# Bias rows first, spatial weights earlier, output weights later, and the gate's tail tile moved forward

## The chip, the core and the metric

The kernel runs on one core of a Trainium2 chip. A core has a matmul engine (PE, with its weight loads shown apart as PEld), a vector engine (DVE), a scalar engine (ACT), GpSimd (POOL), and a queue engine (SP) that only issues transfers. Each works through its own instructions in order, and semaphores tie them together. Matmuls read from on-chip memory (SBUF) and write to accumulator banks (PSUM), which DVE and ACT empty. The metric is the time of one execution on the device in microseconds (us).

## The reference

An attention with eight batches, eight heads, 576 positions and head size 64, followed by a gated layer with a spatial product. Cut to what matters:

```python
scores = scale * q @ k.T
bias = -(cum[:, None] - cum[None, :])          # cum = cumsum(max(s, 0))
scores = where(causal, -1e9, scores + minimum(bias, 0))
x = softmax(scores) @ v                        # heads joined: 576 x 512
h = maximum(x @ w_in, 0)                       # 576 x 1024
u, v = h[..., :512], h[..., 512:]
v_n = (v - mean(v)) / sqrt(var(v) + 1e-6)
v_s = w_spatial @ v_n + b_spatial[:, None]
out = (u * v_s) @ w_out
```

## The kernel before

Every number is held as a sum of two 16-bit halves, so a product is three matmuls. The 576 positions are four tiles of 128 and a tail of 64.

*Attention.* Heads go in pairs, four pairs to a batch, 32 in all. `s_pass` makes the scores of a pair (L303) with DVE's maximum (L307) and ACT's exponential (L313), splits the weights into halves (L322 on ACT, L323 on DVE) and transposes them through SP's queue (L328, `pT`, and `pT('t', p)` for the tail rows). `av_pass` multiplies them with V (L401, and L408 for the tail) and writes the operand `xt` of the second part (L415 on ACT, L416 on DVE). The tail columns of `xt`, from 512 on, come from `avt`, once per batch after its fourth pair. The operands of a pair come by POOL's queue (`raw`) and are split by L241 to L250. Pairs 0 to 2 take their scores from unsplit operands, for which `native_cum` copies the running sums into `kraw` (L128); pair 3 is the first that is split.

*Gated layer, `mlp(b)`.* For each batch 29 steps of PE: five tiles of the gate (`vps`, L443: four full ones and the tail), eight products for u (`ups`, L494), eight spatial products (`sps`: L507 with the full tiles, L509 with the tail's halves `vx`, L510 with the tail's first half and the three bias rows in `VY`), and eight output products (`ops`, L529). A gate tile is emptied by ACT (L459, `hv`), has its mean and variance taken by DVE (L463, L467), is normalized (POOL L469 and L470, DVE L471) and split (ACT L477, DVE L478) into `vn1` and `vn2`. The tail tile is computed in two halves of 64 rows; these exchange their statistics by two transfers on SP (L465, L466), and its result goes by six more (L482 to L484) to `vx` and `VY`. All spatial products of a batch need all five tiles. In batch 0 two gate tiles are begun ahead (`early` is 2); in the others `early` is 0.

*Weights.* They come in chunks of 128 rows. Input and output weights are 64-bit numbers that DVE unpacks in four steps (L167, L168, L170, L174) with one square on ACT (L173); `split_w` makes the halves (ACT L148, then either DVE L150 or ACT L152 and POOL L153). The output weights' chunks come by POOL's queue into one buffer, `wst`. The spatial weights (`load_wsp`) take L148 and L150. `load_wtail` loads the 64 rows of the tail twice into `wsx_st`, splits them into `wx1` and `wx2`, makes three 16-bit pieces of the bias with six steps on DVE (L203, L205, L207) in buffers of tags `ob` and `wst`, and writes them by SP to rows 64 to 66 of `wx2` (L209).

*Order.* PE runs in the order in which the program is written: a plan of (position, step), sorted. Position 2p is the start of pair p, and batch b's 29 steps stand at 8b + 10.3 to 8b + 18.3. The orders of the other engines and the queues are made from the same plan by a scheduler when the program is built; up to position 12.416 a step that is not first waits in its engine's order for the last step that is. The pool of gate, u, spatial and output banks has three, and `hv` has two buffers.

Of the kernel before, what the change touches and what calls it, by code (L numbers as in the profile page):

```python
# [11 lines left out]
AF = mybir.ActivationFunctionType  # L12
ALU = mybir.AluOpType
# [6 lines left out]
SWSP = 1024.0  # L20
SVN = 64.0
# [9 lines left out]
def attn_gated_mlp(ctx, tc, kqT, v, s, w_in, w_spT, b_sp, w_out, outT):  # L31
    nc = tc.nc
# [4 lines left out]
    NH = B * H  # L37
# [8 lines left out]
    NFULL = S // P  # L46
    TAIL = S - NFULL * P
    NC5 = NFULL + 1
# [47 lines left out]
    s_raw, s_pos, cum, zer = (cst[:, i * S:(i + 1) * S] for i in range(4))  # L96
# [14 lines left out]
    engs = (nc.gpsimd.tensor_copy, nc.vector.tensor_copy, nc.scalar.copy)  # L111
# [13 lines left out]
    def native_cum(pair):  # L125
        k = raws[pair // 2, 2 * (pair % 2), "k"]
        for j in range(2):
            engs[(N_C5, N_C5, N_C3, N_C4)[pair]](k[0:NH, j], cum)  # L128

    def init_static(i):  # L130

# [12 lines left out]
    wx1 = cp.tile([P, S], F16, name="wx1")  # L144
    wx2 = cp.tile([P, S], F16, name="wx2")

    def split_w(dst1, dst2, raw, sc, dve):
        nc.scalar.activation(dst1, raw, AF.Copy, bias=0.0, scale=sc)  # L148
        if dve:
            nc.vector.scalar_tensor_tensor(out=dst2, in0=raw, scalar=sc, in1=dst1, op0=ALU.mult, op1=ALU.subtract)  # L150
            return
        nc.scalar.activation(raw, raw, AF.Copy, bias=0.0, scale=sc)  # L152
        nc.gpsimd.tensor_tensor(out=dst2, in0=raw, in1=dst1, op=ALU.subtract)  # L153
# [41 lines left out]
    def load_wtail():  # L195
        s4 = wk.tile([P, S], F32, tag="ob", bufs=2, name="wsx_st")
        nc.sync.dma_start(out=s4[0:TAIL], in_=w_spT[NFULL * P:S])
        nc.sync.dma_start(out=s4[TAIL:2 * TAIL], in_=w_spT[NFULL * P:S])
        split_w(wx1, wx2, s4, SWSP, N_W3 > 4)
        bf = wk.tile([1, S], F32, tag="ob", bufs=2, name="bf")  # L200
        bp = wk.tile([1, 3, S], F16, tag="wst", bufs=1, name="bp")
        nc.sync.dma_start(out=bf, in_=b_sp)
        nc.vector.tensor_scalar(bf, bf, SWSP * SVN / 2048.0, None, op0=ALU.mult)  # L203
        for i in range(3):
            nc.vector.tensor_copy(bp[:, i], bf)  # L205
            if i < 2:
                nc.vector.tensor_tensor(out=bf, in0=bf, in1=bp[:, i], op=ALU.subtract)  # L207
        for i in range(3):
            nc.sync.dma_start(out=wx2[TAIL + i:TAIL + i + 1], in_=bp[:, i])  # L209


    def aux_rows(p):
# [207 lines left out]
    def mlp(b):  # L420
# [11 lines left out]
        def gate_mm(t, cs):  # L432

            tail = t == NFULL
            w = NF // 2 if tail else NF
            if 0 in cs:
                banks[t] = psM.tile([P, 512], F32, tag="M", name=f"vps{b}_{t}")
            ps = banks[t]
            for c in cs:
                for n, (xx, ww) in enumerate(((x1, win1), (x1, win2), (x2, win1))):  # L440
                    for g in range(2 if tail else 1):
                        m = slice(64 * g, 64 * g + 64) if tail else slice(0, P)
                        nc.tensor.matmul(ps[m, 0:w], xx[:, c, t * P:t * P + (m.stop - m.start)],  # L443
                                         ww[:, c, NF + g * w:NF + g * w + w],
                                         start=c == n == 0, stop=c == KC - 1 and n == 2)

        early = N_GP if b == 0 else 0
        if early:
            for c in range(KC - 1):
                for t in range(early):  # L450
                    gate_mm(t, range(c, c + 1))
                yield
        for t in range(NC5):
            tail = t == NFULL
            w = NF // 2 if tail else NF
            gate_mm(t, range(KC - 1 if t < early else 0, KC))
            ps = banks.pop(t)
            hv = wk.tile([P, NF], F32, tag="hv", bufs=2, name=f"hv{b}_{t}")[:, 0:w]
            nc.scalar.activation(hv, ps[:, 0:w], AF.Relu, bias=0.0, scale=VSCALE)  # L459
            st = wk.tile([P, 2, 6], F32, tag="st", bufs=2, name=f"st{b}_{t}")  # L460
            mv = wk.tile([P, 2], F32, tag="mv", bufs=2, name=f"mv{b}_{t}")
            rs = wk.tile([P, 1], F32, tag="rs", bufs=2, name=f"rs{b}_{t}")
            nc.vector.bn_stats(out=st[:, 0], in_=hv)  # L463
            if tail:
                nc.sync.dma_start(out=st[0:64, 1], in_=st[64:128, 0])  # L465
                nc.sync.dma_start(out=st[64:128, 1], in_=st[0:64, 0])  # L466
            nc.vector.bn_aggr(out=mv, in_=st if tail else st[:, 0])  # L467

            nc.gpsimd.tensor_scalar(rs, mv[:, 1:2], 1.0e-6, 1.0 / (SVN * SVN), op0=ALU.add, op1=ALU.mult)  # L469
            nc.gpsimd.tensor_tensor(out=rs, in0=rs, in1=mhalf, op=ALU.pow)  # L470
            nc.vector.tensor_scalar(hv, hv, mv[:, 0:1], rs, op0=ALU.subtract, op1=ALU.mult)  # L471
            if tail:
                d1 = wk.tile([P, w], F16, tag="th", bufs=1, name=f"th{b}")
                d2 = wk.tile([P, w], F16, tag="tl", bufs=1, name=f"tl{b}")
            else:
                d1, d2 = vn1[:, t], vn2[:, t]
            nc.scalar.copy(d1, hv)  # L477
            nc.vector.tensor_tensor(out=d2, in0=hv, in1=d1, op=ALU.subtract)  # L478
            if tail:
                for g in range(2):  # L480
                    m, gs = slice(64 * g, 64 * g + 64), slice(g * w, g * w + w)
                    nc.sync.dma_start(out=vx[0:TAIL, gs], in_=d1[m])  # L482
                    nc.sync.dma_start(out=vy[0:TAIL, gs], in_=d1[m])
                    nc.sync.dma_start(out=vx[TAIL:P, gs], in_=d2[m])  # L484
            yield
# [13 lines left out]
        for hf in range(2):  # L499
            for f in range(FC):  # L500
# [4 lines left out]
                for c in range(NFULL):  # L505
                    for vv, ww in ((vn1, ws1), (vn1, ws2), (vn2, ws1)):
# [6 lines left out]
                                               in1=u[:, f, ts], op0=ALU.mult, op1=ALU.mult)  # L513
# [31 lines left out]
    def at(pos, first, fn, *args):  # L545
        plan.append((pos, len(plan), first, fn, args))
# [19 lines left out]
    at(-20, True, native_sel, 0)  # L566
    at(-19.95, True, prefix_sums)
    at(-19.9, True, native_cum, 0)
    at(-19, True, native_tiles, 1)
    at(-19, True, native_sel, 1)  # L570
    at(-18.9, True, native_cum, 1)
    at(0.5, True, behind, "c", load_raw, 3)
    at(0.6, True, init_static, 0)
    at(0.6, True, behind, "c", fetch_v, 0)
# [4 lines left out]
    at(2.1, True, native_tiles, 2)  # L579
    at(2.1, True, native_sel, 2)  # L580
    at(3, True, native_cum, 2)
    at(5, True, init_static, 1)
    at(5, True, init_static, 2)
# [11 lines left out]
    for c in range(KC):  # L595
        at(2.2 + 1.2 * c, False, fetch_win, 1, c)
        at(4.5 + c, False, fetch_win, 0, c)
        at(6.5 + 0.5 * c, False, load_win, 1, c)
        at(9 + 0.5 * c, False, load_win, 0, c)
        at(11 + 0.4 * c, False, load_wsp, c)  # L600
        at(10.6 + 1.1 * c, False, load_wout, c)
    at(13, False, load_wtail)
    for p in range(NP):
        units([2 * p + k / 3 for k in range(6)], p < 4, s_pass, p)
        at_av = 2 * p + 3.72 if p != 3 else 9.4
        units([at_av, at_av + 0.35], p < 4, av_pass, p)
    for b in range(B):
        poss = [8 * b + 10.3 + 8 / NU * k for k in range(NU)]
        if b == 0:
            pre = [7.3, 8.25, 8.75]  # L610
            units(pre + poss, lambda k: k < len(pre), mlp, b)
        else:
            units(poss, False, mlp, b)
# [54 lines left out]
```

## Time and profile before

| | |
|---|---|
| median of 2 runs | 735.51 us (734.78 to 736.24) |
| profiled execution | 734.97 us |
| its span | 733.2 us |
| PE busy | 600.2 us, 82% |
| DVE busy | 607.0 us, 83% |
| ACT busy | 520.9 us, 71% |
| POOL busy | 226.0 us, 31% |

The profile's page cuts the span into 40 slices of 18.3 us and gives the busy share of each in tenths:

```profile
PE   4474375741998899889989889997999898999997
DVE  8889999795879899789979898999789897985531
POOL 9105465451123432342225331432034322100100
PEclk9788577995999999999999999999999999999999
```

In the first nine slices PE is busy between 30 and 79%, while the weights are loaded and unpacked beside the first pairs, and DVE 70% and more. The tenth slice (about 165 to 183 us) stands out: PE at one tenth, its clock at five. From slice 11 on PE is busy 80 to over 90%, until the last slice.

In the views that follow, a row of the timeline gives start, duration, engine, line, operation, what is written and read, sizes and count; in brackets stands how long the engine was idle before it and what released it. Line numbers are those of the kernel before. After the change lines behind L199 are 4 or 5 higher.

### The profile page before, as it was taken

The page shows a single profiled execution, that of the slowest core. Times are in us where ns is not written, and L with a number is a line of the kernel's source. Part 1 is how long each engine was busy: PE and PEld are TensorE (multiplying, and loading weights), DVE is VectorE, ACT ScalarE, POOL GpSimd, SP SyncE. Part 2 cuts the span into 40 slices and gives each one's busy share as a digit, 9 for nine tenths or more (in the row PEclk, how much of TensorE's full clock was granted, in tenths as well). Part 3 has the DMA queues.
Part 4 walks back from the last instruction along what each step waited for, and adds up shares of the span by engine and source line. Part 5 has one row for each costly group of instructions (what it writes and reads, how often), then busy time and mean ns, then how long its engine had stood idle before and what let it go on. Part 6 is the DMA issues. An engine that isn't in the chain of part 4 may idle for free. (4 is left out here: it accounts for less than half of the span.)

```text
span 733.2 us, 15915 instructions
## 1 busy us (share of the span) xinstructions
PE 600.2 (82%) x5696; PEld 415.7 (57%) x5696; DVE 607.0 (83%) x1660; ACT 520.9 (71%) x1328; POOL 226.0 (31%) x303
## 2 busy tenths in 40 slices
PE   4474375741998899889989889997999898999997
PEld 2152132531774677466756666565756665777576
DVE  8889999795879899789979898999789897985531
ACT  4787578663678777877877868786788787875322
POOL 9105465451123432342225331432034322100100
PEclk9788577995999999999999999999999999999999
DMA  8997747866279597967797698969986979465001
GB/s 224 289 201 132 199 99 198 171 176 156 56 169 202 131 180 181 209 136 160 177 191 161 159 163 184 211 128 167 206 200 123 178 131 179 99 107 123 32 13 64
DMA packets 235101, 114.81 MB, mean 157 GB/s; under 512 B 213471, under 2 KB 216717, under 8 KB 235022
## 3 DMA queue, kind: packets, MB, share of 16 engines
q1 hardware_dynamic: 225726, 78.74, 57.2%
q0 software_dynamic: 9296, 35.07, 16.5%
q8 instruction: 44, 0.72, 0.4%
q14 instruction: 35, 0.29, 0.1%
HBM read 37.28 MB, written 9.44 MB: 64 GB/s over the span
## 5 line engine op out<-in xcount | busy, mean ns | idle before, releaser
L313 ACT ACTIVATE p<-psS,mx 128x256 f32<-128x256 f32 (+3 forms) x256 | 132.9, 524 | 72.5 <-DVE mx L307 57.9
L250 POOL TENSOR_TENSOR QB<-raw,QA 64x288 f16<-64x288 f32 x116 | 118.4, 1049 | 213.2 <-ACT QA L246 175.9
L307 DVE CUSTOM_DVE_ANT_0 psS<-psS,mb 128x512 f32<-128x512 f32 (+2 forms) x320 | 154.3, 493 | 14.2 <-PE psS L303 12.0
L323 DVE SCALAR_TENSOR_TENSOR pb<-p,sm,pb 128x384 f16<-128x384 f32 (+3 forms) x256 | 134.8, 559 | 2.1 <-ACT pb L322 1.6
L322 ACT ACTIVATE pb<-p,sm 128x384 f16<-128x384 f32 (+3 forms) x256 | 122.8, 555 | 7.0 <-DVE sm L318 3.2
L443 PE MATMUL vps<-win,xt 128*128 128x512 f16 (+1 forms) x576 | 105.2, 354 | 18.6 <-ACT ob L532 9.6
L303 PE MATMUL psS<-KA,QA 128*128 128x128 f16 (+1 forms) x348 | 82.9, 312 | 40.4 <-ACT p L313 37.7
L507 PE MATMUL sps<-ws,vn 128*128 128x288 f16 x768 | 106.7, 289 | 10.8 <-DVE g L512 7.2
L494 PE MATMUL ups<-xt,win 128*128 128x288 f16 x768 | 106.6, 293 | 0.6 <-ACT u L497 0.4
L529 PE MATMUL ops<-g,wo 128*128 128x288 f16 x768 | 101.8, 286 | 1.1 <-DVE g L515 1.0
L507 PEld LDWEIGHTS <-vn 128*128 128x128 f16 x768 | 74.6, 99 | 35.9 <-issue 13.2
L494 PEld LDWEIGHTS <-win 128*128 128x128 f16 x768 | 75.6, 100 | 28.7 <-issue 5.1
L303 PE MATMUL psS<-KB,QB 128*128 128x128 f16 (+1 forms) x348 | 89.3, 306 | 1.1 <-DMA QB<-QA 1.1
L529 PEld LDWEIGHTS <-wo 128*128 128x128 f16 x768 | 74.5, 98 | 24.3 <-issue 2.0
L443 PEld LDWEIGHTS <-xt 128*128 128x128 f16 (+1 forms) x576 | 48.4, 103 | 67.8 <-issue 29.4
L401 PE MATMUL av<-pT,V 128*64 128x128 f16 (+2 forms) x960 | 64.0, 282 | 19.7 <-DMA pT<-pb 19.6
L401 PEld LDWEIGHTS <-V 128*64 128x64 f16 x960 | 52.0, 114 | 37.2 <-issue 26.6
L469 POOL TENSOR_SCALAR rs<-mv 128x1 f32<-128x1 f32 x40 | 12.5, 312 | 134.1 <-DVE mv L467 124.0
L303 PEld LDWEIGHTS <-QA 128*128 128x128 f16 x348 | 30.6, 103 | 39.1 <-issue 29.1
L313 ACT ACTIVATION_READ_ACCUMULATOR p<-psS,mx 128x1 f32 x256 | 51.0, 199 | 0.0
L514 ACT CAST g<-g 128x288 f16<-128x288 f32 x64 | 27.1, 429 | 30.4 <-DVE g L512 29.1
L303 PEld LDWEIGHTS <-QB 128*128 128x128 f16 x348 | 30.2, 103 | 30.1 <-issue 16.3
(121 smaller groups left out, 923.4 us busy)
## 6 DMA issues: line engine op xcount, KB each, us to landing
raw<-in_kqT_dram POOLq DMA_DIRECT2D x29, 576.0 KB, 4.7
out_dram<-ob SPq DMA_DIRECT2D x32, 288.0 KB
vraw<-in_v_dram POOLq DMA_DIRECT2D x16, 512.0 KB, 6.9
KA<-kh SPq DMA_DIRECT2D x29, 144.0 KB
KB<-kh SPq DMA_DIRECT2D x29, 144.0 KB
QB<-QA SPq DMA_DIRECT2D x29, 144.0 KB
wst<-in_w_in_dram POOLq DMA_DIRECT2D x8, 512.0 KB, 7.4
vraw<-in_v_dram POOLq DMA_DIRECT2D x16, 128.0 KB, 6.9
```

The lines of the kernel that those rows point to most:

```text
L250: nc.gpsimd.tensor_tensor(out=QB[i][hi, j, c], in0=raw[hi, j, c], in1=QA[i][hi, j, c], op=ALU.subtract)
L303: nc.tensor.matmul(ps[m, c0:c0 + w], U[i][:, g, q0:q0 + n], T[i][:, g, k0:k0 + w], start=st, stop=not st)
L307: nc.vector.tensor_tensor_reduce(out=ps[:, c0:c0 + w], in0=ps[:, c0:c0 + w], in1=mask, op0=ALU.add, op1=ALU.min, scale=-0.125, scalar=3.0e ...
L313: nc.scalar.activation(p32, ps[:, c0:c0 + w], AF.Exp, bias=mx[:, col:col + 1], scale=-1.0, accum_out=sm[:, acc:acc + 1])
L322: nc.scalar.activation(dst[:, off:off + w], p32, AF.Copy, bias=0.0, scale=sm[:, col:col + 1])
L323: nc.vector.scalar_tensor_tensor(out=dst[:, n + off:n + off + w], in0=p32, scalar=sm[:, col:col + 1], in1=dst[:, off:off + w], op0=ALU.mul ...
L401: nc.tensor.matmul(dst, V[i][:, jc, h + j], rhs, start=jc == n == 0 and q0 > 0, stop=jc == 3 and n == 2)
L443: nc.tensor.matmul(ps[m, 0:w], xx[:, c, t * P:t * P + (m.stop - m.start)], ww[:, c, NF + g * w:NF + g * w + w], start=c == n == 0, stop=c ...
L494: nc.tensor.matmul(ps[:, 0:TH], ww[:, c, fs], xx[:, c, ts], start=n == 0, stop=n == 3 * KC - 1)
L507: nc.tensor.matmul(ps[:, 0:TH], vv[:, c, fs], ww[:, c, ts], start=n == 0, stop=False)
L514: nc.scalar.copy(g1[:, f, ts], g32)
L529: nc.tensor.matmul(ps[:, 0:TH], ww[:, f, ms], gg[:, f, ts], start=n == 0, stop=n == 3 * FC - 1)
```

## The change

- `native_cum`: for pairs 0 and 1 one of the two copies (j = 0) moves from DVE to ACT. (`engs` is POOL, DVE, ACT; `N_C5` is 1.)
- The bias becomes a step of its own, `load_bias`, at position -18.8 instead of 13: its load, six steps and three writes are all issued by POOL.
- `load_wtail` stands at 11.5 instead of 13. Its second half is written for rows 0 to 63 only, since rows 64 to 66 already hold the bias.
- `load_wsp` stands at 9.9 + 0.4c instead of 11 + 0.4c, `load_wout` at 12 + 0.8c instead of 10.6 + 1.1c.
- The gate's tile order is [first `early` tiles, tail, remaining full tiles] instead of the tail last: 0, 1, 4, 2, 3 in batch 0, and 4, 0, 1, 2, 3 in batches 1 to 7.

```diff
-            engs[(N_C5, N_C5, N_C3, N_C4)[pair]](k[0:NH, j], cum)
+            engs[(2 - j, 2 - j, N_C3, N_C4)[pair]](k[0:NH, j], cum)
...
-        split_w(wx1, wx2, s4, SWSP, N_W3 > 4)
+        nc.scalar.activation(wx1, s4, AF.Copy, bias=0.0, scale=SWSP)
+        nc.vector.scalar_tensor_tensor(out=wx2[0:TAIL], in0=s4[0:TAIL], scalar=SWSP, in1=wx1[0:TAIL], op0=ALU.mult,
+                                       op1=ALU.subtract)
+
+    def load_bias():
         bf = wk.tile([1, S], F32, tag="ob", bufs=2, name="bf")
         bp = wk.tile([1, 3, S], F16, tag="wst", bufs=1, name="bp")
-        nc.sync.dma_start(out=bf, in_=b_sp)
-        nc.vector.tensor_scalar(bf, bf, SWSP * SVN / 2048.0, None, op0=ALU.mult)
+        nc.gpsimd.dma_start(out=bf, in_=b_sp)
+        nc.gpsimd.tensor_scalar(bf, bf, SWSP * SVN / 2048.0, None, op0=ALU.mult)
...
-            nc.sync.dma_start(out=wx2[TAIL + i:TAIL + i + 1], in_=bp[:, i])
+            nc.gpsimd.dma_start(out=wx2[TAIL + i:TAIL + i + 1], in_=bp[:, i])
...
-        for t in range(NC5):
+        for t in list(range(early)) + [NFULL] + list(range(early, NFULL)):
...
+    at(-18.8, True, load_bias)
...
-        at(11 + 0.4 * c, False, load_wsp, c)
-        at(10.6 + 1.1 * c, False, load_wout, c)
-    at(13, False, load_wtail)
+        at(9.9 + 0.4 * c, False, load_wsp, c)
+        at(12 + 0.8 * c, False, load_wout, c)
+    at(11.5, False, load_wtail)
```

SP's queue from the tail's weights on, before the change (`pT_1591` and `pT('t', 6)` belong to pair 6):

```order
L197 DMA wsx_st<-in_w_spT_dram 64x576
L198 DMA wsx_st<-in_w_spT_dram 64x576
L482 DMA vx_651<-th_1218 64x256
L483 DMA VY_110<-th_1218 64x256
L484 DMA vx_651<-tl_1219 64x256
L482 DMA vx_651<-th_1218 64x256
L483 DMA VY_110<-th_1218 64x256
L484 DMA vx_651<-tl_1219 64x256
L328 DMA_TRANSPOSE pT_1591<-pb_1505 128x20x128
L202 DMA bf<-in_b_sp_dram 1x576
L328 DMA_TRANSPOSE pT('t', 6)_1603<-pb_6_1593 128x10x128
L209 DMA wx_123<-bp 1x16x36 x3
```

The same place after it (`pT_1271` and `pT('t', 5)` belong to pair 5):

```order
L197 DMA wsx_st<-in_w_spT_dram 64x576
L198 DMA wsx_st<-in_w_spT_dram 64x576
L251 DMA QB_102<-QA_75 64x1152
L486 DMA vx_663<-th_1157 64x256
L487 DMA VY_110<-th_1157 64x256
L486 DMA vx_663<-th_1157 64x256
L487 DMA VY_110<-th_1157 64x256
L488 DMA vx_663<-tl_1158 64x256 x2
L332 DMA_TRANSPOSE pT_1271<-pb_1167 128x20x128
L332 DMA_TRANSPOSE pT('t', 5)_1283<-pb_5_1273 128x10x128
```

The bias transfers have left the queue, and the tail's weights and tile moved from behind pair 5's transposes to ahead of them.

DVE around the last gating of batch 0, `g_0_31` (the product of u and the eighth spatial product), before:

```order
L366 TENSOR_TENSOR mx_1696<-mx_1696 128x1
L416 SCALAR_TENSOR_TENSOR xt_1_1297<-av_1922,xt_1_1296 128x512
L317 TENSOR_SCALAR sm_1697<-sm_1697 128x4
L318 RECIPROCAL sm_1697<-sm_1697 128x4
L369 TENSOR_TENSOR sm_1697<-sm_1697 128x1
L241 CAST kh_2735<-raw_2098 64x1152
L317 TENSOR_SCALAR sm_1697<-sm_1697 128x1
L512 SCALAR_TENSOR_TENSOR g_0_31_1998<-sps_31_1983,u_652 128x288
```

And after:

```order
L168 SCALAR_TENSOR_TENSOR wt<-wst,wt 128x512
L321 TENSOR_SCALAR sm_1686<-sm_1686 128x4
L516 SCALAR_TENSOR_TENSOR g_0_31_1998<-sps_31_1983,u_664 128x288
L311 ISA psS_2006,mx_2002<-psS_2006,mb 128x128
L311 ISA mx_2002 128x1
L170 SCALAR_TENSOR_TENSOR wt<-wst,wt 128x512
L322 RECIPROCAL sm_1686<-sm_1686 128x4
L245 CAST kh_2735<-raw_2098 64x1152
L373 TENSOR_TENSOR sm_1686<-sm_1686 128x1
L311 ISA psS_2006,mx_2002<-psS_2006,mb 128x384
L311 ISA mx_2002 128x1
L174 SCALAR_TENSOR_TENSOR wt<-wst,wt 128x512
```

The unpacking of the fourth chunk of output weights (L167 to L174) stood around the second gating, `g_0_10`, and now ends behind the last one.

PE at the start of batch 1's gate, before (`ops_31` is the last output product of batch 0; `xt_1` is the stationary operand):

```order
L529 MATMUL ops_31_2292<-g_0_653,wo_119 128x288
L443 LDWEIGHTS xt_1_1296
L443 MATMUL vps_0_2317<-win_116,xt_1_1296 128x512
L443 LDWEIGHTS xt_1_1296
L443 MATMUL vps_0_2317<-win_117,xt_1_1296 128x512
```

And after:

```order
L533 MATMUL ops_31_2292<-g_0_665,wo_119 128x288
L447 LDWEIGHTS xt_1_1299
L447 MATMUL vps_4_2317<-win_116,xt_1_1299 64x256
L447 LDWEIGHTS xt_1_1299
L447 MATMUL vps_4_2317<-win_116,xt_1_1299 64x256
```

The tail tile `vps_4` took the place of the first full tile `vps_0`; scores of a later pair stand between the tiles as before.

More of the change, by code (lines that the diff above doesn't have):

```diff
@@ L198, in load_wtail @@
         nc.sync.dma_start(out=s4[TAIL:2 * TAIL], in_=w_spT[NFULL * P:S])
-        split_w(wx1, wx2, s4, SWSP, N_W3 > 4)
+        nc.scalar.activation(wx1, s4, AF.Copy, bias=0.0, scale=SWSP)
+        nc.vector.scalar_tensor_tensor(out=wx2[0:TAIL], in0=s4[0:TAIL], scalar=SWSP, in1=wx1[0:TAIL], op0=ALU.mult,
+                                       op1=ALU.subtract)
+    def load_bias():
         bf = wk.tile([1, S], F32, tag="ob", bufs=2, name="bf")
         bp = wk.tile([1, 3, S], F16, tag="wst", bufs=1, name="bp")
-        nc.sync.dma_start(out=bf, in_=b_sp)
-        nc.vector.tensor_scalar(bf, bf, SWSP * SVN / 2048.0, None, op0=ALU.mult)
+        nc.gpsimd.dma_start(out=bf, in_=b_sp)
+        nc.gpsimd.tensor_scalar(bf, bf, SWSP * SVN / 2048.0, None, op0=ALU.mult)
         for i in range(3):
-            nc.vector.tensor_copy(bp[:, i], bf)
+            nc.gpsimd.tensor_copy(bp[:, i], bf)
             if i < 2:
-                nc.vector.tensor_tensor(out=bf, in0=bf, in1=bp[:, i], op=ALU.subtract)
+                nc.gpsimd.tensor_tensor(out=bf, in0=bf, in1=bp[:, i], op=ALU.subtract)
         for i in range(3):
-            nc.sync.dma_start(out=wx2[TAIL + i:TAIL + i + 1], in_=bp[:, i])
+            nc.gpsimd.dma_start(out=wx2[TAIL + i:TAIL + i + 1], in_=bp[:, i])
     def aux_rows(p):
```

## The prediction

> **What bounds the kernel now.** I read the busy time by stage first, then the matmul engine's timeline in the stage that stands out, then what its releasers were doing. A row of the first view gives the stage in us, its length, and each engine's busy time (with instruction counts), then the granted clock, DMA share and GB/s.
>
> ```profile
> 157.30:180.20 22.90, 1.13 (x6) 0.34 (x5) 16.64 (x31) 10.16 (x22) 9.69 (x10) 0.60 0.73 164
> 169.90:203.85 33.95, 23.14 (x204) 16.71 (x205) 23.21 (x59) 16.46 (x41) 7.23 (x8) 0.76 0.39 85
> 219.50:297.50 78.00, 72.27 (x714) 50.63 (x712) 69.18 (x200) 61.94 (x162) 25.90 (x35) 0.98 0.84 174
> ```
>
> From batch 1 on (third row) PE is busy 72.3 of 78.0 us and DVE 69.2: PE sets the pace with DVE close behind, so a few us lost on either are hard to win back. The exception is the first row, where PE works 1.1 of 22.9 us. What it waited for:
>
> ```profile
> 159.04 0.28 PE L507 MATMUL sps<-ws,vn 128*128 128x288 f16 x1 [1.72 <-ACT ws L148]
> 161.27 0.41 PE L507 MATMUL sps<-ws,vn 128*128 128x288 f16 x2 [1.94 <-DVE ws L150]
> 172.32 0.40 PE L509 MATMUL sps<-wx,vx 128*128 128x288 f16 x1 [10.65 <-DMA vx<-tl]
> 180.19 0.40 PE L510 MATMUL sps<-wx,VY 67*128 67x288 f16 x1 [7.46 <-DMA wx<-bp]
> ...
> 143.81 3.81 SPq L328 DMA_TRANSPOSE pT<-pb  x1
> 164.76 0.54 SPq L197 DMA_DIRECT2D wsx_st<-in_w_spT_dram  x1
> 169.17 0.59 SPq L484 DMA_DIRECT2D vx<-tl x1
> 175.89 3.02 SPq L209 DMA_DIRECT2D wx<-bp  x3
> 180.62 0.55 POOL L158 DMA_DIRECT2D wst<-in_w_out_dram  x1 [6.16 <-DMA wx<-bp]
> ```
>
> The first spatial product of batch 0 waits four times, 1.72 + 1.94 + 10.65 + 7.46 = 21.8 us: for the last spatial weights, for the tail tile of the gate, for the bias rows. All four are inputs that the change makes earlier. The last row is POOL, whose load of the fourth chunk of output weights waits 6.16 us for the buffer that the bias rows hold; that goes too.
>
> **The hole.** In SP's queue, as the rows in the part on the change show, the bias is gone, and the tail's weights and tiles now stand ahead of pair 5's transposes (143.81) instead of behind them and one of pair 6's (164.76): some 20 us earlier. If nothing else were late, PE would win 21.8 us. But in the hole DVE works off a backlog (16.64 of 22.90 us), and that work stays. So I count DVE:
>
> ```profile
> L203 DVE TENSOR_SCALAR bf<-bf x1: 448/448/448, 174.9 to 174.9; 1x576 f32<-1x576 f32 x1
> L205 DVE CAST bp<-bf x3: 448/449/449, 175.4 to 177.9; 1x576 f16<-1x576 f32 x3
> L207 DVE TENSOR_TENSOR bf<-bf,bp x2: 747/747/747, 175.9 to 177.2; 1x576 f32<-1x576 f32 x2
> ...
> 186.73 0.68 DVE L174 SCALAR_TENSOR_TENSOR wt<-wst,wt 128x512 f32<-128x512 f32 x1
> 203.85 0.44 DVE L512 SCALAR_TENSOR_TENSOR g<-sps,u 128x288 f32<-128x288 f32 x1
> 189.50 1.15 POOL L153 TENSOR_TENSOR wo<-wt,wo 128x512 f16<-128x512 f32 x1 [8.32 <-ACT wt L152]
> 201.74 1.63 PE L529 MATMUL ops<-g,wo 128*128 128x288 f16 x12
> ```
>
> From 169.90 to the last gating of batch 0 at 203.85 (second row of the first view) DVE idles 33.95 - 23.21 = 10.7 us, and the bias takes 0.45 + 3 x 0.45 + 2 x 0.75 = 3.3 us that go to POOL. DVE can thus reach that gating at most 14.0 us sooner. A new lateness eats half of it. The fourth chunk of output weights was unpacked 17 us ahead of that gating (L174 at 186.73). Now, with the chunks moved to 12 and later, its last step on DVE stands behind it, and the first output product needs all four chunks. Sum: the gating at 203.85 - 14.0 = 189.9; some 3 us to the end of L174, since the rows between are of the kinds that take 0.3 to 0.7 us; some 2.5 us for the two steps on ACT and the one on POOL (1.15 us); and 1 us for a chunk's load that lands late, since one buffer serves all four and the next load waits until it is read. The chunk is ready near 196.4. Before, the twelve matmuls that use it ended at 203.4 (201.74 + 1.63). That leaves **7.0 us gained**. Bounds: 14.0, if the chunk is not late; 0, if the tail's weights, now loaded in the middle of the transposes, only move the wait. The fourth full tile, now last in batch 0's gate, has the eight u products to hide in, as the tail had; I cost its later place at nothing.
>
> **The gate of batches 1 to 7.** There `early` is 0, so the new order starts with the tail tile, not third but first. The tail tile reads columns 512 on of xt, which are the last to be made (L415 and L416 on avt), and the fifth matmul already needs DVE's half:
>
> ```profile
> 219.52 2.75 PE L443 MATMUL vps<-win,xt 128*128 128x512 f16 x12
> 224.22 0.41 DVE L416 SCALAR_TENSOR_TENSOR xt<-avt,xt 128x256 f16<-128x256 f32 x1
> 224.70 2.75 PE L443 MATMUL vps<-win,xt 128*128 128x512 f16 x12 [1.99 <-ACT ob L532]
> 249.57 0.22 PE L303 MATMUL psS<-KA,QA 128*128 128x128 f16 x1 [2.41 <-ACT p L313]
> ...
> 610.96 2.75 PE L443 MATMUL vps<-win,xt 128*128 128x512 f16 x12
> 615.06 0.42 DVE L416 SCALAR_TENSOR_TENSOR xt<-avt,xt 128x256 f16<-128x256 f32 x1
> 616.28 2.75 PE L443 MATMUL vps<-win,xt 128*128 128x512 f16 x12 [2.13 <-ACT ob L532]
> ...
> 680.05 1.24 PE L443 MATMUL vps<-win,xt 128*128 128x512 f16 x5
> L416 DVE SCALAR_TENSOR_TENSOR xt<-avt,xt x1: 414/414/414, 678.8 to 678.8; 128x256 f16<-128x256 f32 x1
> ```
>
> In batch 1 PE would stand from 219.52 to 224.63, 5.1 us, in place of the 1.99 us that it now waits after its first tile: 3.1 us lost. In batch 6 it is 4.5 against 2.13: 2.4 us. In batch 7 the tail is ready (679.2) before PE (680.05): nothing. Neither ACT's nor DVE's order ahead of these copies changes, so nothing brings them sooner. Part is given back: PE waits 2.41 us at 249.57 anyway, for scores that DVE and ACT hand on, and if PE is 3.1 us later there, DVE is late by less. DVE handles the 256-wide scores at
>
> ```profile
> 227.28 0.27 PE L303 MATMUL psS<-KA,QA 128*128 128x256 f16 x1
> 228.16 0.41 DVE L307 CUSTOM_DVE_ANT_0 psS<-psS,mb 128x256 f32<-128x256 f32 x1
> ```
>
> After the change these scores end near 224.63 + 1.3 (rest of the tail) + 0.4 + 2.75 + 0.3 = 229.4, so DVE slips by 1.2 us and so does all behind it. I take batches 2 to 5 like batch 1, 1.2 us each, and batch 6 whole, since no such wait follows there: 5 x 1.2 + 2.4 = **8.4 us lost**; bounds 0 and 5 x 3.1 + 2.4 = 17.9. A stall may also slow the clock:
>
> ```profile
> 105.18 0.37 PE L303 MATMUL psS<-KA,QA 128*128 128x256 f16 x1 [4.71 <-ACT p L313]
> 105.56 5.32 PE L443 MATMUL vps<-win,xt 128*128 128x512 f16 x12
> ```
>
> After an idle of 4.71 us twelve such matmuls took 5.32 instead of 2.75 us, 2.6 more; after 1.99 (224.70) they took 2.75. Stalls of 4.5 to 5.1 lie at the former, but DVE lags there anyway, so I take **2 us** for the six and keep 0 and 15 as ends. The Trainium skill ("TensorE: Matmul & The Clock Gate", What's actually happening) says the gate drops to half rate after an idle window of about 3.4 us; by that rule stalls of this length can go cold, depending on where the free-running window lies; the pair of rows agrees.
>
> **The start, and what moves without a price.**
>
> ```profile
> 8.49 1.15 ACT L246 CAST QA<-raw 64x1152 f16<-64x1152 f32 x1 [1.86 <-DMA raw<-in_kqT_dram]
> 1.76 0.78 POOL L231 DMA_DIRECT2D raw<-in_kqT_dram  x1
> L128 DVE COPY kraw<-cst x4: 531/696/1704, 6.2 to 8.7; 64x576 f32<-64x576 f32 x4
> 63.94 6.50 POOL L250 TENSOR_TENSOR QB<-raw,QA 64x288 f16<-64x288 f32 x4 [22.98 <-ACT QA L246]
> 99.00:135.00 36.00, 19.89 (x147) 10.20 (x146) 35.49 (x81) 25.28 (x57) 26.77 (x30) 0.81 0.75 171
> ```
>
> Two of DVE's four copies go to ACT, which so far waits 1.86 us for a load right behind: at the median of 0.70 us they are 1.4 us of DVE. Against that stands the load of the bias, the first of its four DMAs, which POOL now issues ahead of pair 3's operands and so delays them by one issue of some 0.8 us. I take **0.8 us gained**, bounds -1 and 2. The six bias steps have no row on POOL; nearest is L153 at 1.15 us (512 columns), so about 7 us, and three more DMA issues of 0.8. POOL's idle 23 us ahead of 63.94 cover them; without that cover the loads of input weights behind them would come 9 us later. I cost them at nothing. Between 99 and 135 DVE has no room (35.49 of 36.00 us): the spatial weights' steps move into it and the first chunks of output weights out of it, kinds of 0.4 to 0.8 us in like number, which I cost at nothing, with 2 us either way as the bound; pair 4's and 5's work stands behind them.
>
> The Trainium skill ("SBUF — State Buffer", Who interferes with whom) says that GpSimd and DVE share a port pair as an exclusive lock; by that rule the six steps could hold DVE up by at most their own 7 us, which no row here prices.
>
> **Sum**, against the profiled execution's 734.97 us (0.5 below the median of 735.51): 734.97 - 7.0 - 0.8 + 8.4 + 2.0 = 737.6, taken as **738 us**.
>
> **Rivals.** (a) Faster: batches 1 to 6 absorb their stall, and the fourth chunk is not late: 735.0 - 14.0 - 0.8 = 720. For it: 10.7 us of idle DVE. Against it: PE busy 93% behind. (b) Slower: the stall at each gate stays whole, and the clock falls at each: 735.0 - 7.0 - 0.8 + 17.9 = 745, and with 2.6 us for the slow clock in half of the six, 753. It decides once a batch loses over 2.5 us. (c) The hole only moves, to the tail's weights or to the fourth full tile, now last: 735.0 - 0.8 + 8.4 + 2.0 = 745.
>
> **Numbers.** Forecast 0.50, (a) 0.18, (b) 0.22, (c) 0.10. A measurement of this kernel tells about 2% (14.7 us) from no change. Half of (a) falls below 720.8, nearly half of (b) above 750.2, and 0.02 from the forecast's edges at either side: faster 0.11, same 0.78, slower 0.11. Range 722 to 750, which cuts the far halves of (a) and (b).
>
> **What would show it.** The waits on vx and wx at 172 and 180 gone, bias casts on POOL before 45 us; a PE wait for wo or for DVE's last unpacking at the first output product; in batches 1 to 6 a PE wait of 4.5 to 5.1 us on the tail of xt at the gate's start, none in batch 7; period of batch 1 at 79 to 80 us against 78.0. I am wrong if the gate's stall is absent, or if the first output product comes over 12 us sooner.

## The result, and the profile after

The changed kernel takes 771.27 us (median of 2 runs, 769.95 to 772.59), against 735.51 us before: a ratio of 1.049, 95% interval 1.040 to 1.058. It is slower by some 36 us, and above the predicted range (722 to 750 us). The profiled execution took 772.59 us, its span is 770.8 us. In the experiments below, executions in a slower state are left out of the ratios, but not of the medians.

Where the time came in is read from PE's timeline: the start of each batch's gate (after the change, the first tail matmul, once its wait is over).

| gate of batch | before, us | after, us | later by |
|---|---|---|---|
| 1 | 219.52 | 221.16 | 1.6 |
| 2 | 297.51 | 304.05 | 6.5 |
| 3 | 375.76 | 390.89 | 15.1 |
| 4 | 455.80 | 473.23 | 17.4 |
| 5 | 533.87 | 562.50 | 28.6 |
| 6 | 610.96 | 648.28 | 37.3 |
| 7 | 680.05 | 718.02 | 38.0 |

Batch 0 ends about where it ended. The loss, 35.7 of 37.6 us, lies between the gates of batches 1 and 6. For that stretch here are busy time by stage (length, then PE, PEld, DVE, ACT and POOL busy, clock, DMA share, GB/s) and the waits of PE and of DVE (us in total, times, longest). Before:

```profile
219.52:610.96 391.44, 355.84 (x3562) 251.35 (x3560) 347.46 (x994) 309.29 (x806) 128.02 (x171) 1.00 0.86 171
PE psS L303 <- ACT p L313: 14.6, 11, 2.4
PE vps L443 <- ACT ob L532: 7.4, 4, 2.5
PE sps L507 <- DVE g L512: 7.2, 5, 2.3
DVE mv L467 <- DMA st<-st: 2.4, 2, 1.5
```

And after:

```profile
221.16:648.28 427.12, 365.84 (x3560) 254.20 (x3560) 350.11 (x997) 310.63 (x806) 115.77 (x168) 0.97 0.75 157
PE psS L307 <- ACT p L317: 13.8, 12, 1.8
PE sps L511 <- DVE g L516: 12.4, 5, 4.5
PE ups L498 <- ACT hv L463: 11.9, 9, 1.8
PE vps L447 <- DVE xt L420: 8.8, 5, 1.9
PE vps L447 <- ACT xt L419: 8.0, 5, 3.2
PE ops L533 <- DVE g L519: 3.5, 4, 1.8
DVE mv L471 <- DMA st<-st: 9.5, 5, 3.0
```

PE idles 61.3 us in place of 35.6, and is busy 10.0 us longer with the same matmuls at a lower granted clock: it stands at one half six times, for 27.3 us in all (in the kernel before once, for 3.4 us). One of the six:

```profile
305.45:312.28 6.83, 6.06 (x29) 2.94 (x30) 3.95 (x7) 3.09 (x10) 1.30 (x2) 0.50 1.07 229
```

DVE and ACT do the same work as before. The wait for the tail columns of xt is there (8.8 + 8.0 = 16.8 us at the gates of batches 1 to 5, where the gate before waited 7.4 for emptied banks), as predicted. At the gate of batch 6 it looks like this:

```profile
648.28 0.41 PE L447 MATMUL vps<-win,xt 128*64 128x256 f16 x4 [3.40 <-ACT xt L419]
649.76 1.96 PE L447 MATMUL vps<-win,xt 128*64 128x256 f16 x20 [1.07 <-DVE xt L420]
```

But the first u products now also wait 11.9 us for emptied gate tiles (`hv`), and the spatial and output products 8.7 us more for DVE's gating. One batch shows how the second wait arises. Timelines of ACT, DVE, SP and PE at the gate of batch 4:

```profile
477.45 0.38 ACT L463 ACTIVATE hv<-vps 128x256 f32<-128x256 f32 x1 [0.90 <-PE vps L447]
481.64 0.60 ACT L463 ACTIVATE hv<-vps 128x512 f32<-128x512 f32 x1 [1.65 <-PE vps L447]
493.03 1.07 ACT L463 ACTIVATE hv<-vps 128x512 f32<-128x512 f32 x2
...
479.51 3.53 SPq L332 DMA_TRANSPOSE pT('t', 20)_5897<-pb  x1
483.13 0.54 SPq L469 DMA_DIRECT2D st<-st  x1
488.96 0.26 DVE L471 BATCH_NORM_AGGREGATE mv<-st 128x2 f32<-128x12 f32 x2 [3.03 <-DMA st<-st]
493.67 1.63 PE L498 MATMUL ups<-xt,win 128*128 128x288 f16 x12 [1.82 <-ACT hv L463]
```

The tail tile fills one hv buffer at 477.45, the first full tile the other at 481.64. Both are held until DVE has the tail's exchanged statistics, at 488.96: the tail's by the exchange itself, the full tile's because its aggregation stands right behind the tail's on DVE (the count of 2 in that row). Of the wait for the exchange 3.7 us come ahead of its first transfer: DVE has the tail's own statistics at 479.46, but the transfer is issued at 483.13, behind a transpose in SP's queue. No gate tile is emptied for 11 us, and PE has its banks full.

In batch 0 the waits on `vx` and `wx` (10.65 and 7.46 us before) and on the spatial weights are gone. These stand in their place, on PE and on POOL:

```profile
141.20 0.42 PE L498 MATMUL ups<-xt,win 128*128 128x288 f16 x2 [3.33 <-ACT win L148]
146.72 0.42 PE L498 MATMUL ups<-xt,win 128*128 128x288 f16 x1 [5.10 <-POOL win L153]
195.94 0.30 PE L533 MATMUL ops<-g,wo 128*128 128x288 f16 x1 [2.80 <-POOL wo L153]
201.32 0.66 PE L533 MATMUL ops<-g,wo 128*128 128x288 f16 x2 [5.08 <-ACT wo L148]
203.28 0.42 PE L533 MATMUL ops<-g,wo 128*128 128x288 f16 x1 [1.30 <-POOL wo L153]
...
42.97 0.80 POOL L263 DMA_DIRECT2D vraw<-in_v_dram  x1 [14.10 <-DVE V L271]
54.87 0.55 POOL L158 DMA_DIRECT2D wst<-in_w_in_dram  x1 [5.08 <-DMA wx<-bp]
```

The output weights are late by 9.2 us in all, and now the input weights are late too: u waits 8.4 us for them. Two things differ ahead of them. POOL's load of the sixth chunk was held up until 54.87 (40.42 before), and on DVE the last unpacking of the last two chunks ends behind steps of the spatial weights, which stood behind it before (113.71):

```profile
120.39 0.94 DVE L150 SCALAR_TENSOR_TENSOR ws<-wsp_st,ws 128x576 f16<-128x576 f32 x1
121.42 0.65 DVE L174 SCALAR_TENSOR_TENSOR wt<-wst,wt 128x512 f32<-128x512 f32 x1
135.39 0.74 DVE L150 SCALAR_TENSOR_TENSOR ws<-wsp_st,ws 128x576 f16<-128x576 f32 x1
139.27 1.21 DVE L174 SCALAR_TENSOR_TENSOR wt<-wst,wt 128x512 f32<-128x512 f32 x1
```

### The profile page after: what moved, and what is told of

Its sections match the earlier page's. It is cut to its first block, busy times and chain, and to the rows that moved or that the text cites. A ratio compares the mean times of both kernels' runs of the same rounds, so it can differ in the third digit from the quotient of the medians.

```text
span 770.8 us, 15949 instructions
## 1 busy us (share of the span) xinstructions
PE 614.9 (80%) x5696; PEld 419.7 (54%) x5696; DVE 599.8 (78%) x1652; ACT 523.6 (68%) x1330; POOL 236.2 (31%) x313
## 3 DMA queue, kind: packets, MB, share of 16 engines
q0 software_dynamic: 9424, 35.07, 15.1%
## 5 line engine op out<-in xcount | busy, mean ns | idle before, releaser
L317 ACT ACTIVATE p<-psS,mx 128x384 f32<-128x384 f32 (+3 forms) x256 | 132.9, 524 | 101.9 <-DVE mx L311 89.9
L254 POOL TENSOR_TENSOR QB<-raw,QA 64x288 f16<-64x288 f32 x116 | 125.2, 1106 | 221.1 <-ACT QA L250 167.1
L327 DVE SCALAR_TENSOR_TENSOR pb<-p,sm,pb 128x384 f16<-128x384 f32 (+3 forms) x256 | 132.6, 549 | 6.9 <-ACT pb L326 6.7
L447 PE MATMUL vps<-win,xt 128*128 128x512 f16 (+1 forms) x576 | 114.9, 387 | 27.6 <-ACT xt L419 11.4
L498 PE MATMUL ups<-xt,win 128*128 128x288 f16 x768 | 104.2, 289 | 20.3 <-ACT hv L463 11.9
L533 PE MATMUL ops<-g,wo 128*128 128x288 f16 x768 | 104.4, 288 | 13.0 <-ACT wo L148 5.1
L447 PEld LDWEIGHTS <-xt 128*128 128x128 f16 (+1 forms) x576 | 52.0, 116 | 84.1 <-issue 19.5
L307 PEld LDWEIGHTS <-QA 128*128 128x128 f16 x348 | 30.0, 102 | 37.6 <-issue 27.0
L536 ACT ACTIVATE ob<-ops 128x288 f32<-128x288 f32 x64 | 24.9, 409 | 29.6 <-PE ops L533 15.2
```

Source lines behind the costliest of these rows:

```text
L254: nc.gpsimd.tensor_tensor(out=QB[i][hi, j, c], in0=raw[hi, j, c], in1=QA[i][hi, j, c], op=ALU.subtract)
L307: nc.tensor.matmul(ps[m, c0:c0 + w], U[i][:, g, q0:q0 + n], T[i][:, g, k0:k0 + w], start=st, stop=not st)
L317: nc.scalar.activation(p32, ps[:, c0:c0 + w], AF.Exp, bias=mx[:, col:col + 1], scale=-1.0, accum_out=sm[:, acc:acc + 1])
L327: nc.vector.scalar_tensor_tensor(out=dst[:, n + off:n + off + w], in0=p32, scalar=sm[:, col:col + 1], in1=dst[:, off:off + w], op0=ALU.mul ...
L498: nc.tensor.matmul(ps[:, 0:TH], ww[:, c, fs], xx[:, c, ts], start=n == 0, stop=n == 3 * KC - 1)
L533: nc.tensor.matmul(ps[:, 0:TH], ww[:, f, ms], gg[:, f, ts], start=n == 0, stop=n == 3 * FC - 1)
```

## The experiments

Ratios are to the kernel before on the same chip in the same session; medians of different sessions compare only roughly. "Batches 1 to 6" is the distance between those gates in the profile.

| run | edit | median us | ratio (95%) | batches 1 to 6 |
|---|---|---|---|---|
| before | | 735.51 | | 391.4 |
| after | | 771.27 | 1.049 (1.040 to 1.058) | 427.1 |
| e1 | after, tail last in batches 1 to 7 | 736.17 | 0.998 (0.991 to 1.005) | 393.8 |
| e2 | before, tail first in batches 1 to 7 | 777.73 | 1.061 (1.054 to 1.068) | 429.4 |
| e3 | after, tail second there | 740.71 | 1.012 (1.002 to 1.022) | 400.5 |
| e4 | after, tail third there | 747.65 | 1.019 (1.014 to 1.024) | 406.9 |
| e5 | after, own hv buffer for the tail | 761.58 | 1.032 (1.017 to 1.046) | 427.0 |
| e6 | after, tail without its wait for xt | 762.34 | 1.034 (1.020 to 1.047) | 425.4 |
| e7 | after, no exchange of statistics | 764.73 | 1.038 (1.026 to 1.049) | 422.9 |
| e11 | e5 and e6 | 741.64 | 1.008 (1.003 to 1.012) | 401.0 |
| e12 | e5, e6 and e7 | 750.60 | 1.015 (1.004 to 1.027) | 412.9 |
| e8 | e1, output weights back | 730.66 | 0.990 (0.985 to 0.995) | 396.3 |
| e10 | e8, bias in another buffer | 727.36 | 0.984 (0.971 to 0.998) | 392.9 |
| e13 | e10, own hv buffer for the tail | 736.86 | 1.003 (0.998 to 1.009) | 395.3 |
| e14 | e10, spatial weights back | 736.33 | 1.002 (0.994 to 1.009) | 389.6 |
| e15 | e10, spatial weights at 10.6 | 735.61 | 0.993 (0.989 to 0.998) | 389.7 |

### Which part of the change: e1 and e2

e1 takes back the gate's order in batches 1 to 7; e2 does that part alone.

```diff
-        for t in list(range(early)) + [NFULL] + list(range(early, NFULL)):
+        for t in ((0, 1, NFULL, 2, 3) if early else range(NC5)):
```

> All of the change, but in batches 1 to 7 the gate takes its tail tile last, as before; batch 0 keeps it third. In the changed kernel's trace the gate of batch 1 starts 1.6 us later than before and that of batch 7 38.0 us later, so 36 us come in between. Theory A (the tail tile first in batches 1 to 6 is the loss): 735 us, the same as before, with gate starts 78 to 80 us apart again. Rival B (the moved weights and bias leave DVE and the queues late, and the batches carry that along): 765 to 771 us.

```diff
-        for t in range(NC5):
+        for t in (range(NC5) if early else (NFULL, 0, 1, 2, 3)):
```

> The kernel before, with one edit: in batches 1 to 7 the gate's tail tile comes first; batch 0 and all weights and bias are as before. Theory A (that order is the loss): 735.5 + 36 = 771 us. Rival B (the moved weights and bias are): 735 to 740 us. My own prediction's price for that order, 8 to 10 us, would give 745 us.

Theory A holds in both directions: without the order the loss is gone (0.998), and the order alone makes 6.1% (some 45 us, more than the 36 expected). The rest of the change is worth about nothing by itself, 0.998, though it removed 21.8 us of waits.

### How much of it is the tail's place: e3 and e4

The tail stands second (0, 4, 1, 2, 3), or third (0, 1, 4, 2, 3), in batches 1 to 7.

```diff
-        for t in list(range(early)) + [NFULL] + list(range(early, NFULL)):
+        for t in ((0, 1, NFULL, 2, 3) if early else (0, NFULL, 1, 2, 3)):
...
+        for t in (0, 1, NFULL, 2, 3):
```

> The changed kernel with the tail tile second instead of first in batches 1 to 7 (0, 4, 1, 2, 3). PE has one full tile of 2.75 us before it needs the tail of xt, so of the waits of 2.6 to 4.7 us at the gate about 2 stay. In SP's order the six transfers of the tail tile still stand ahead of the next pair's operands KA, KB and QB. Theory A1 (the wait of PE for xt is what costs): 3 us less in each of six batches, about 753 us. Theory A2 (the tail tile's exchange and transfers, ahead of other work in SP's queue and in DVE's order, cost as much again): 760 to 768 us.

> The changed kernel with the tail tile third in all batches (0, 1, 4, 2, 3), as in its batch 0. PE has two full tiles, over 5 us, before the tail of xt: no wait there. In SP's order the exchange of statistics still stands ahead of the next pair's operands, the six transfers behind them. Theory A1 (the wait for xt is what costs): 735 us, as with the tail last. Theory A2 (exchange and transfers in the queues cost as well): 742 to 755 us, between the tail second and the tail last.

One full tile ahead of the tail takes away about 30 of the 36 us, far more than the 18 us that I had for the wait alone: e3 lies below both theories, e4 in A2's range, and the third place isn't better than the second. In the third DVE waits for something else, the next pair's transfer of KB, before it may refill the one buffer `kh`: 29.4 us in 14 waits between the gates of batches 1 and 6, against 7.7 us before. So A2's queues can count as well, but with some 10 us, and the control below shows that so much may come of another order alone.

### Which wait: e5, e6, e7

All three keep the tail first. e5 gives its emptied tile a buffer of its own, e6 lets it read other columns of xt, e7 leaves the exchange out.

```diff
-            hv = wk.tile([P, NF], F32, tag="hv", bufs=2, name=f"hv{b}_{t}")[:, 0:w]
+            hv = wk.tile([P, w], F32, tag="hvt" if tail else "hv", bufs=1 if tail else 2, name=f"hv{b}_{t}")
```

> The changed kernel (tail tile first in batches 1 to 7), with one edit: the tail tile has a buffer of its own (256 columns) for its emptied gate tile, so that the two hv buffers serve the four full tiles alone. Between the gates of batches 1 and 6 the first products of u waited 11.9 us for ACT's emptying of the last gate tiles, 9 waits, which the kernel before did not have. Theory H (the tail tile, waiting for its exchange of statistics, holds one of the two hv buffers and so delays the full tiles behind it): these waits go, 10 to 15 us less, 756 to 761 us. Rival (DVE's order is what delays them, since DVE stands at the tail's statistics): the waits stay, 768 to 772 us.

```diff
-                        nc.tensor.matmul(ps[m, 0:w], xx[:, c, t * P:t * P + (m.stop - m.start)],
+                        nc.tensor.matmul(ps[m, 0:w], xx[:, c, (448 if tail and b else t * P):(448 if tail and b else t * P) + (m.stop - m.start)],
```

> The changed kernel, where in batches 1 to 7 the gate's tail tile reads columns 448 to 511 of xt instead of 512 to 575: the same matmuls on other rows, so PE needn't wait there for the last columns to be written. (This changes the result: the tail rows of the gate are those of rows 448 to 511.) Theory A1 (the wait for the last columns of xt is the loss, with what follows from it: DVE late, clock down): the batches come back to 78 to 80 us and the time to 737 to 745 us. Theory A2 (only the 17 us of direct waits between the gates of batches 1 and 6 go, partly for waits that the kernel before had; the exchange, the hv buffers and the transfers stay): 753 to 762 us.

```diff
-            if tail:
+            if tail and not b:
                 nc.sync.dma_start(out=st[0:64, 1], in_=st[64:128, 0])
                 nc.sync.dma_start(out=st[64:128, 1], in_=st[0:64, 0])
-            nc.vector.bn_aggr(out=mv, in_=st if tail else st[:, 0])
+            nc.vector.bn_aggr(out=mv, in_=st if tail and not b else st[:, 0])
```

> The changed kernel without the two transfers that exchange the tail tile's statistics in batches 1 to 7; each half of the tail is normalized by its own 256 columns. (This leaves a part of the computation out: the tail's mean and variance over all 512 columns.) DVE stood 9.5 us at that exchange between the gates of batches 1 and 6, against 2.4 us before. Theory X (the exchange, with little to do ahead of it on DVE, is the larger part of the loss): 745 to 755 us. Theory A1 (the wait for xt is): 762 to 770 us.

Each gives about 7 to 10 us by the medians, with intervals that overlap that of the change, and in the profiles the batches hardly get shorter (427.0, 425.4 and 422.9 us, against 427.1). Some 5.9 us of the gain lie ahead of the gate of batch 1 there, which starts at 215.2 to 215.3 instead of 221.16, without the slow step on POOL that the last section shows. The traces say why the batches stay. e5, between the gates of batches 1 and 6:

```profile
215.28:642.28 427.00, 371.64 (x3561) 256.46 (x3562) 349.51 (x997) 312.44 (x806) 116.30 (x168) 0.95 0.76 157
PE psS L307 <- ACT p L317: 24.3, 10, 5.9
PE vps L447 <- ACT xt L419: 17.5, 6, 4.3
PE vps L447 <- DVE xt L420: 7.8, 5, 1.7
```

and e6:

```profile
215.32:640.74 425.42, 369.35 (x3561) 256.93 (x3560) 348.89 (x996) 310.70 (x807) 123.60 (x169) 0.96 0.74 157
PE ups L498 <- ACT hv L463: 18.4, 5, 4.8
PE ops L533 <- DVE g L519: 14.6, 5, 5.8
DVE mv L471 <- DMA st<-st: 19.8, 5, 5.1
```

With the hv wait gone (e5), PE waits longer for xt: 26.4 us at the gates of batches 1 to 6, in place of 21.3 (these rows of e5 count six gates of ACT's and five of DVE's, those of the change five of each), and the scores wait 24.3 us for ACT in place of 13.8. PE idles 55.4 us instead of 61.3, but is busy 5.8 us longer at a clock of 0.95. With the xt wait gone (e6), DVE stands longer at the tail's exchange (19.8 instead of 9.5), u waits 18.4 us for hv instead of 11.9, and the output products 14.6 us for DVE's gating instead of 3.5; PE idles 56.1 us and is busy 3.5 us longer. What one wait gives up, others and the clock take. For e5 neither side was right: the waits for hv went, as theory H says, and the batches stayed, so its 761.6 us, at the edge of H's range, don't bear H out. e6 lies at the upper end of A2's range, e7 in A1's: DVE no longer waits for the exchange, and the waits for xt (20.3 us) remain.

### Both at once: e11 and e12

> The changed kernel (tail tile first in batches 1 to 7) with two edits together: the tail tile reads columns 448 to 511 of xt, so that it waits for nothing there (which changes the result: the tail rows of the gate are those of rows 448 to 511), and it has a buffer of its own for its emptied tile. Each edit alone gave 10 us of 36. Theory M (each of the two waits alone is long enough to set the batch: with one gone, the other grows): together they give far more than 20 us, 737 to 745 us, with batches 78 to 80 us apart. Rival S (the two are worth 10 us each and the rest lies elsewhere, in queues or DVE's order): 748 to 754 us.

> As the run before it (the tail tile reads columns 448 to 511 and has a buffer of its own), and also without the exchange of the tail's statistics in batches 1 to 7 (each half is normalized by its own 256 columns, which leaves that part out). Theory M: 735 to 740 us, as with the tail last; what is left to the run before it is DVE's stand at the exchange, 2 to 8 us. Rival S: 738 to 746 us, 10 us below the run before it.

e11 is theory M's: 741.6 us, 30 us below the change, where the edits alone gave 9 and 10. Between the gates of batches 1 and 6 it is clearer still: 26.1 us less, where e5 alone gave 0.1 and e6 alone 1.7. Its waits between the gates of batches 1 and 6:

```profile
212.94:613.95 401.01, 360.71 (x3561) 252.22 (x3560) 350.87 (x992) 308.78 (x800) 131.58 (x167) 0.99 0.78 167
PE vps L447 <- ACT ob L536: 11.6, 5, 3.1
PE ups L498 <- ACT hv L463: 2.1, 2, 1.6
```

What is left at the gate is the wait for free banks, which the kernel before has too (7.4 us), and the clock is back at 0.99. e12 came out against both theories: 9 us slower than e11, though it leaves work out. Without the exchange the order made for DVE is another. At the gates of batches 4 and 5 the refill of `kh` stands ahead of DVE's copy of the tail of xt, where in e11 it stands behind it, and DVE waits at its refills: 34.6 us in 14 waits between those gates, where e11 has 1.9 us.

### The start: e8, e10, e14 and e15

All have the tail last in batches 1 to 7. e8 puts the output weights back, e10 also moves the bias pieces to a buffer that is free then; e14 and e15 are e10 with the spatial weights at two later places.

```diff
-        at(12 + 0.8 * c, False, load_wout, c)
+        at(10.6 + 1.1 * c, False, load_wout, c)
...
-        bp = wk.tile([1, 3, S], F16, tag="wst", bufs=1, name="bp")
+        bp = wk.tile([1, FC, S], F16, tag="g1", bufs=1, name="bp")
```

> The kernel with the tail tile last again in batches 1 to 7 (as in the first experiment), and with the output weights back at positions 10.6 + 1.1c. In the first experiment's profile the first output products of batch 0 wait 2.8 + 5.1 + 1.3 = 9.2 us for the third and fourth chunk of output weights. Theory W (the later place of the chunks gave that part of the hole back): these waits fall to under 2 us and the gate of batch 1 starts 5 to 9 us sooner, near 208 us; 5 to 9 us less than in the first experiment. Rival (DVE is full there and the work only moves): the u or spatial products of batch 0 are late by as much, and the time is that of the first experiment within 2 us.

> The tail tile last again in batches 1 to 7, the output weights back at 10.6 + 1.1c, and the bias pieces in the buffer of g1, which is free until batch 0's gating, instead of in the one that the chunks of input and output weights come through. In the profiles with the bias made first, POOL's load of an input-weight chunk waits 5.1 us for the bias rows (54.9 instead of 40.4 us before), and the u products of batch 0 wait 5 to 8 us for input weights, which they did not before. Theory P (the bias holds the chunks' buffer): the load comes back to 40 to 45 us, the waits of u for input weights shrink, 3 to 8 us less than with the output weights back alone (730.7 us). Rival (POOL's and ACT's other work delays the input weights): the same within 2 us.

```diff
-        at(9.9 + 0.4 * c, False, load_wsp, c)
+        at(11 + 0.4 * c, False, load_wsp, c)
...
+        at(10.6 + 0.4 * c, False, load_wsp, c)
```

> As the version with the tail last in batches 1 to 7, the output weights back and the bias in g1's buffer (727.4 us), with the spatial weights back at 11 + 0.4c. In the changed kernel DVE unpacks the last two chunks of input weights at 121.4 and 139.3 us (112.7 and 113.7 before), with the third and fourth step of the spatial weights ahead of them, and the first u products wait 8.4 us for input weights; with the output weights back and the bias moved they still wait 3.7 + 1.6 us. Theory O (the spatial weights, moved ahead of the last input weights in DVE's order, are what makes these late): the waits of u for input weights fall under 1 us, and spatial products of batch 0 wait 2 to 4 us for spatial weights, as before; time within 4 us of 727 us. Rival B (the bias on POOL and its buffer make the input weights late): u still waits 4 us or more for them.

> The same with the spatial weights at 10.6 + 0.4c, right behind the last input weights (10.5). Theory O: u waits under 1 us for input weights, spatial products wait for no weights, the gate of batch 1 starts 2 to 5 us sooner than with them at 9.9 (209.5 us), and the time is 722 to 727 us. Rival B: u still waits 4 us or more, 727 us or more.

In e8 no output product waits for weights any more (9.2 us in e1), and it is 5.5 us below e1 by the medians, though the two intervals overlap. But the gate of batch 1 starts at 212.63, only 3.4 us sooner than e1's 215.98: the spatial products start at 168.2 instead of 162.6, so DVE's full stretch gave part of it back, as the rival says. In e10 the weights' load no longer waits for the bias rows (POOL's timeline has two loads at 47.18, where e8 has them at 50.03 and 55.66). Both come later than the 40 to 45 us expected, and u still waits 3.7 + 1.6 us for input weights, instead of 5.6 + 1.4 in e8. The gate of batch 1 starts at 209.50, and the median is 3.3 us lower. The two intervals overlap, so P is borne out by the load, not by the time. e10 lies below the kernel before, at 0.984 (0.971 to 0.998), as e8 and e15 do by less; none of them is clear of 2%.

e14 and e15 settle what makes u wait: with the spatial weights behind the last input weights, u waits for input weights nowhere, in either. Theory O is right there, rival B is not. But its time is wrong, for the wait moves. PE's waits for weights in batch 0, e14 and then e15:

```profile
PE sps L511 <- DVE ws L150: 6.1, 2, 5.0
PE sps L511 <- ACT ws L148: 5.1, 1, 5.1
...
PE sps L511 <- ACT ws L148: 12.0, 1, 12.0
PE sps L511 <- DVE ws L150: 0.8, 1, 0.8
```

The spatial products wait 11.2 and 12.8 us for the spatial weights, where I expected 2 to 4 and none, and the gate of batch 1 starts at 216.66 and 220.33 instead of 209.50. The change's place for the spatial weights costs u 5 to 8 us and is still the best of the three by the gate of batch 1; in time the intervals of e10 and e15 overlap.

### A control: e13

The edit is that of e5, on e10.

> The version with the tail tile last in batches 1 to 7, the output weights back at 10.6 + 1.1c and the bias pieces in g1's buffer (727.4 us), with a buffer of its own for the tail's emptied tile. A control on theory M: with the tail last, no full tile comes behind it that could want the hv buffer, and PE waited for hv nowhere in its batches 1 to 5. Theory M expects no difference: 724 to 731 us. Rival (a third hv buffer helps in any order): 715 to 722 us, with the batches 1 to 2 us shorter.

The rival falls, but theory M's "no difference" does too: 736.9 us, 9.5 more than e10 by the medians (4.8 us between the two profiled executions, and 1.003 against 0.984 as ratios). PE's order is the same in both; that of DVE, ACT and SP is not, since the scheduler makes it from the same plan with another buffer. A mere reshuffle of these three can thus cost some 5 to 10 us here. That is a warning for this section: the 9 and 10 us of e5 and e6 singly, and the differences between e3 and e4 and between e11 and e12, are of that size and can't be put down to one edit. The 36 to 45 us of the tail's place (e1, e2) and the 30 us of e11 are well outside it.

## Why the prediction was wrong

- **The step that failed** is "The gate of batches 1 to 7". It predicted "8.4 us lost", at most 17.9; the batches lost 36. The order was read rightly (tail first, not third) and so was the wait for the last columns of xt: 3.4 us in the mean of batches 1 to 5, 4.5 in batch 6 (3.40 + 1.07), against 4.5 to 5.1 predicted, and none in batch 7. Two things were wrong. "Part is given back" assumed that DVE slips by 1.2 us of 3.1; nothing was given back: PE's waits for the scores, where it was to be, are 13.8 us in place of 14.6, since the next scores stand behind the stalled tail in PE's order and DVE idles with PE (DVE busy 350.1 of 427.1 us, against 347.5 of 391.4). The period of batch 1 became 82.9 us, where 79 to 80 were predicted. And the tail's buffers were left out of the sum: with the tail first, its exchange holds an hv buffer and DVE while four full tiles wait behind it. I had "the eight u products to hide in" in mind for batch 0 and did not ask what stands behind the tail in the others.
- **The clock**, "2 us", was mis-sized: PE was busy 10.0 us longer between the gates of batches 1 and 6 alone. PE was busy in 24.0 of the 27.3 us at half clock, and in all of the 3.4 before. By an estimate from the prediction's own rows (5.32 against 2.75 us for the same twelve matmuls), about half of that is lost: 12.0 - 1.7 = 10.3 us, which is the 10.0. It needed no stall of 4.5 us: the stretch of half clock that starts at 223.53 stands behind two stalls of 0.69 and 1.85 us. The upper bound of 15 held the sum.
- **Rival (b)**, the stall whole and the clock low, was the right side, and its turning point (over 2.5 us a batch) was passed: 7.1 us a batch. Its ceiling of 753 us was too low, because it held that one wait and nothing that follows it.
- **The hole.** The waits on vx and wx went, with the bias on POOL before 45 us, and the output weights were late, as said. "7.0 us gained" was too high. The twelve matmuls that use the fourth chunk were to end near 196.4; they ended at 198.9 in e1 and 203.7 (203.28 + 0.42) in the changed kernel's profile. In four other executions with the same start (e1, e4, e6 and e7) the gate of batch 1 begins at 215.2 to 216.0, 3.5 to 4.3 us sooner than before, against 7.8 predicted with the start's 0.8. The profile of the changed kernel has 5 us more, from one slow step on POOL (below).
- **What was costed at nothing** at the start was not free. The spatial weights, moved into DVE's full stretch with "2 us either way", push the last input weights back there, and PE waits 8.4 us for these where it had not (e14 and e15 take that away). They are worth their place all the same: later ones cost 11.2 and 12.8 us. The bias on POOL held up a chunk's load, as the step's own proviso said ("without that cover"): its third piece stands behind a load of V that waits 14.10 us, and holds the buffer of the weights' chunks. In time that was small, 3.3 us between e8 and e10, within their intervals.
- **Rivals (a) and (c)**: (a) is refuted. (c), the hole only moves, is most of what happened at the start, though not to the places that it names (the tail's weights, the fourth full tile): of 21.8 us that went, 17.6 (8.4 + 9.2) came back as waits for input and output weights.
- **The signs of being wrong** don't bear on what failed. The gate's stall was there. The first output product started 9.7 us sooner in the changed kernel (192.00 instead of 201.74), not 12; in e1, with the same start, 14.5 us sooner (187.22), but there it then waits 9.2 us for weights.

What stays open is how much of the 36 us each of the two waits would carry in an order that is held fixed: every edit here let the scheduler reorder DVE, ACT and SP.

## What to carry to other kernels

Before a step is moved to the front of a group, ask two things of it: which of its inputs is made last, and what it holds while it waits (a buffer, a bank, the head of an in-order engine), for all that now stands behind it. A stall on the bound engine is given back only if the engines that feed it have work that doesn't come from it. And where taking one wait away moves the time little, take both away together before calling it harmless: between the gates e5 and e6 gave 0.1 and 1.7 us, e11 gave 26.1.

## What the runs showed of the hardware that was not expected

One product on POOL, `QB` from `raw` (64x288), has a median of 0.73 us in the changed kernel and took 10.84 us there once and 10.85 in e3, at the same place of the program, and at most 4.25 us in every other profile. POOL's timeline, the changed kernel and then e1, four such products each:

```profile
67.70 17.27 POOL L254 TENSOR_TENSOR QB<-raw,QA 64x288 f16<-64x288 f32 x4 [12.28 <-ACT QA L250]
...
67.47 6.57 POOL L254 TENSOR_TENSOR QB<-raw,QA 64x288 f16<-64x288 f32 x4 [12.74 <-ACT QA L250]
```

and busy time of the stretch, in the same two:

```profile
68.00:85.00 17.00, 7.68 (x69) 5.01 (x69) 17.00 (x33) 10.89 (x21) 16.97 (x4) 0.50 0.57 114
68.00:85.00 17.00, 5.83 (x64) 4.39 (x64) 16.17 (x26) 10.21 (x19) 11.27 (x12) 0.60 0.60 158
```

In the slow one DVE is busy all 17.00 us, without a gap; in e1 it has 0.8 us of gaps. The load of V and the next weights behind that product come 8 to 9 us later, and the gate of batch 1 some 5 us. Where DVE does pause, the two change places. In e1, behind its gap of 0.8 us, POOL runs its next four products without a break, and a DVE step that takes 0.67 us in the changed kernel takes 3.68 beside them:

```profile
74.91 2.80 POOL L254 TENSOR_TENSOR QB<-raw,QA 64x288 f16<-64x288 f32 x4
74.58 3.68 DVE L170 SCALAR_TENSOR_TENSOR wt<-wst,wt 128x512 uint32<-128x512 uint32 x1
```

The Trainium skill ("SBUF — State Buffer", Who interferes with whom) calls the port pair that GpSimd shares with DVE an exclusive lock; the trace agrees so far as POOL stood while DVE never paused, and DVE while POOL ran its four products, but no run here shows the lock itself, nor why 2 of the 14 profiles with the bias on POOL have the long step.
